# An attention and two-MoE kernel on one core: the first MoE's sums laid out by model dimension, the second MoE's tokens staged by a table

## The chip, the core and the metric

The kernel runs on one core of a Trainium2 chip. A core has TensorE (PE, with its weight loads shown apart as PEld), VectorE (DVE), ScalarE (ACT), GpSimd (POOL) and SyncE (SP), which issues most transfers. Matrix products read SBUF and write PSUM, which has eight banks of 128 x 512 numbers. The metric is the device time of one execution in microseconds (us).

## The reference

```python
# attention without a softmax over pairs: q, k, v are (4, 8, 576, 64)
q_s = softmax(q, axis=-1);  k_s = softmax(k, axis=2)
x = (q_s @ (k_s^T @ v))            # per head; then (2304 tokens, 512)
# first MoE: 4 experts, d_model 512, d_ff 1024, all tokens through all experts
p = probs / (probs.sum(-1) + 1e-9)
for e in range(4):
    out += p[:, e:e + 1] * (relu(x @ w1[e]) @ w2[e])
# second MoE layer: one expert, d_ff 2048
result = elu(out @ w_in) @ w_out   # w_in and w_out are given in float64
```

## The kernel before, in words

Every factor is split into a high and a low part (`fp32r`), and each product is three matmuls: high x high, high x low, low x high. The first expert of the first MoE ("unit 0") is computed plainly, beside the attention: for a block of 256 tokens `first` makes one 128-wide slice of the hidden layer, `second` adds it into the sums of the block, and `evacuate` moves the finished sums into `accs` in SBUF, scaled by the token's probability. Hooks (`at(n, ...)`) put the attention's and other work between these matmuls; one hook comes after every 2048 columns.

The other three experts and the second MoE are 30 *steps* `i`, each of half an expert (index `s`, 0 to 9) and a third of the tokens (index `b` = `i` mod 3, 768 tokens in two halves `th` of TB = 384). Steps with `s` < 6 are the first MoE, those with `s` >= 6 the second. A step runs a Strassen-like scheme: the first layer is 14 products (7 for each of two halves `fp`; 6 matmuls of 384 columns each, line 1177) in four PSUM banks A, B, C, D, with sums of banks on VectorE (lines 1474 and 1485) and ScalarE. Of steps with `s` < 5 or `s` > 6 the second layer is seven products as well; they run one step later, in the places PLACES between the first-layer products (`second_product` for the first MoE, `turned_product` for the second). Steps with `s` = 5 and 6 have a plain second layer (`chunk` and `group`). The steps of `s` = 5 are 15, 16 and 17; each step's second layer runs in the step after it.

In `second_product` the hidden activations are the stationary operand, 128 tokens at a time, and the weights move: 3 token tiles x 6 matmuls of 256 columns for one product. The sums stand as (tokens, model dimension), and a token's probability is a scalar per partition: VectorE adds `probability x sum` into `accs` with three instructions of 128 x 256 (line 1425), and one of the seven products' parts goes through ScalarE (1420) and POOL (1421) instead. `chunk` does the same with 512 columns (lines 1263 to 1265, 1270). The second MoE needs its input as (model dimension, tokens), so `turn_steps` transposes `accs` on TensorE (line 970, 8 transposes and 2 copies by ScalarE for 256 tokens; 9 such pairs), makes the seven sums of quarters that its products need, splits them (`emit`, ScalarE, VectorE, POOL) and stores them to DRAM (`xs`), from where each step loads its operands (`ring_load`). `drain` pops one piece of up to two such streams after each first-layer product.

Every engine runs its instructions in the order in which the program writes them. VectorE's order within a step is thus fixed: the bank sums (1474 after product 2, 1485 after product 4), the ReLU parts (1355, 1360, 1369), the adds of the second products, the splitting of the next weights (777, 782, 783, 823) and the conversion of float64 weights (487 to 506). In the trace a first-layer product of one half `fp` cannot start overwriting a bank before the ReLU of the earlier content has read it.

## Time and profile before

| | before |
|---|---|
| time, median of 3 runs | 1180.96 us (1180.72 to 1181.03) |
| the profiled execution's own time | 1180.01 us |
| its span | 1178.2 us |
| TensorE matmuls, busy | 1161.9 us in 7551 |
| VectorE / ScalarE / POOL busy | 883.9 / 656.1 / 604.1 us |
| granted clock of TensorE | 1.00 over the whole span |

The span is what the trace covers; the execution's own time has 1.8 us around it. Matmul records overlap, since one matmul's end is modelled while the next already streams: what a matmul costs is the distance from its start to the next one's start, and a stretch can be 100% busy and still hold short waits.

### The profile page before, as it was taken

To read this page: it belongs to the slowest core of one execution; us is meant where nothing else is said; L and a number is where in the kernel's file an instruction comes from. 1 tells how busy PE (TensorE), PEld (TensorE's weight loads), DVE (VectorE), ACT (ScalarE), POOL (GpSimd) and SP (SyncE) were. 2 spreads that over 40 slices of the span, in tenths; PEclk is the share of its full clock that TensorE was granted. 3 is DMA by queue.
4 is the path that set the end of the run, shared out by engine and by line. 5 is a ranking of instruction groups with operands and counts; after the bars stand their busy time and mean duration, and the time that the engine had idled before them with its cause. 6 is when DMAs were issued, how large, how long until landed. Compare 5 with 4: busy or idle time off the path is not lost.

```text
span 1178.2 us, 21091 instructions
## 1 busy us (share of the span) xinstructions
PE 1161.9 (99%) x7551; PEld 1113.6 (95%) x7551; DVE 883.9 (75%) x1533; ACT 656.1 (56%) x1410; POOL 604.1 (51%) x582
## 2 busy tenths in 40 slices
PE   8999999999999999999999999999999999999998
PEld 6889898889999999999999999998999999999998
DVE  7878887555787787787787786576566779879876
ACT  7554544236455455455455453356767766767763
POOL 6522543027468468468468463246534645645643
PEclk9999999999999999999999999999999999999999
DMA  9446666846767767767777658798985465565462
GB/s 270 144 144 191 192 211 222 287 166 224 259 233 251 259 233 251 258 233 250 253 239 251 241 208 311 259 340 279 335 320 188 181 230 198 196 229 198 176 242 108
DMA packets 150345, 272.76 MB, mean 231 GB/s; under 512 B 12640, under 2 KB 74848, under 8 KB 150240
## 3 DMA queue, kind: packets, MB, share of 16 engines
q1 hardware_dynamic: 148512, 268.26, 66.1%
q10 hardware_dynamic: 1728, 3.15, 0.8%
q8 instruction: 60, 0.98, 0.3%
q14 instruction: 45, 0.37, 0.1%
HBM read 225.22 MB, written 46.14 MB: 230 GB/s over the span
## 4 chain that ended last, share of the span: by engine, by line
PE 80%; DVE 5%; ACT 2%; issue 1%; POOL 1%; DMA 0%; DVEq 0%; POOLq 0%; ACTq 0%
PE o L1403 19%; PE m L1177 17%; PE h L1177 17%; PE o L1312 8%; PE h L1035 4%; PE o L1035 4%; PE o L1283 1%; PE o L1284 1%; PE o L1285 1%; PE o L1264 1%; PE o L1265 1%; PE o L1263 1%; DVE accs L1321 1%; PE o L970 1%; DVE w1s L777 1%
## 5 line engine op out<-in xcount | busy, mean ns | idle before, releaser
L1177 PE MATMUL m<-xh,w1s 128*128 128x384 f32 x840 | 245.9, 337 | 1.3 <-DVE h L1474 0.8
L1177 PE MATMUL h<-xh,w1s 128*128 128x384 f32 x840 | 244.8, 337 | 1.9 <-DVE half L1233 0.9
L1177 PEld LDWEIGHTS m<-xh,w1s 128*128 128x128 f32 x840 | 154.2, 188 | 6.1 <-DVE gt L1360 2.2
L1177 PEld LDWEIGHTS h<-xh,w1s 128*128 128x128 f32 x840 | 154.8, 188 | 5.1 <-DVE half L1233 1.5
L1177 PE MATMUL h<-xl,w1s 128*128 128x384 f32 x420 | 140.7, 335 | 0.0
L1177 PE MATMUL m<-xl,w1s 128*128 128x384 f32 x420 | 140.6, 335 | 0.0
L1035 PE MATMUL o<-w2t,hpa 128*128 128x512 f32 x432 | 117.1, 399 | 1.0 <-ACT hpa L1066 0.5
L1035 PE MATMUL h<-xh,w1t 128*128 128x256 f32 (+1 forms) x512 | 110.9, 295 | 0.0
L1403 PE MATMUL o<-w2g,xh 128*128 128x256 f32 x540 | 90.4, 282 | 0.0
L1035 PEld LDWEIGHTS o<-w2t,hpa 128*128 128x128 f32 x432 | 75.7, 189 | 14.8 <-DVE hpa L1067 1.9
L1035 PEld LDWEIGHTS h<-xh,w1t 128*128 128x128 f32 x512 | 85.0, 189 | 4.8
L1403 PE MATMUL o<-w2g,hpa 128*128 128x256 f32 x540 | 89.0, 282 | 0.0
L1403 PE MATMUL o<-w2g,xl 128*128 128x256 f32 x540 | 87.3, 282 | 0.0
L815 POOL TENSOR_TENSOR w2g<-r,w2g 128x512 fp32r<-128x512 f32 x56 | 74.8, 1344 | 24.2 <-ACT w2g L814 24.2
L1425 DVE SCALAR_TENSOR_TENSOR accs<-o,pn,accs 128x256 f32<-128x256 f32 x180 | 75.7, 475 | 14.7 <-PE o L1403 14.1
L1177 PEld LDWEIGHTS h<-xl,w1s 128*128 128x128 f32 x420 | 79.2, 189 | 0.3
L1177 PEld LDWEIGHTS m<-xl,w1s 128*128 128x128 f32 x420 | 78.9, 188 | 0.5
L1403 PEld LDWEIGHTS o<-w2g,xh 128*128 128x128 f32 x540 | 78.0, 190 | 0.1
L1035 PE MATMUL h<-xl,w1t 128*128 128x256 f32 (+1 forms) x256 | 77.0, 301 | 0.5 <-DVE xl L413 0.5
L1403 PEld LDWEIGHTS o<-w2g,hpa 128*128 128x128 f32 x540 | 76.1, 190 | 0.1
L1403 PEld LDWEIGHTS o<-w2g,xl 128*128 128x128 f32 x540 | 75.7, 190 | 0.1
L1201 POOL TENSOR_TENSOR hpa<-gt,hpa 128x384 fp32r<-128x384 f32 x28 | 28.5, 1020 | 75.3 <-ACT hpa L1199 75.3
(357 smaller groups left out, 2960.3 us busy)
## 6 DMA issues: line engine op xcount, KB each, us to landing
xh<-xs SPq DMA_DIRECT2D x210, 384.0 KB, 5.5
xl<-xs SPq DMA_DIRECT2D x210, 384.0 KB, 6.1
r<-in_w_dram SPq DMA_DIRECT2D x56, 256.0 KB, 4.8
xs<-xh SPq DMA_DIRECT2D x21, 384.0 KB, 4.6
xs<-xl SPq DMA_DIRECT2D x21, 384.0 KB, 4.4
xs<-stage SPq DMA_DIRECT2D x29, 256.0 KB, 5.1
r<-scratch SPq DMA_DIRECT2D x24, 256.0 KB, 4.2
xs<-gt SPq DMA_DIRECT2D x21, 256.0 KB, 4.5
```

Of the source, the lines that this page charges most:

```text
L777: eng.tensor_tensor(out=dst(k, 1), in0=src(k), in1=dst(k, 0).bitcast(F32), op=ALU.subtract)
L815: nc.gpsimd.tensor_tensor(out=t[:, 1], in0=src, in1=t[:, 0].bitcast(F32), op=ALU.subtract)
L970: nc.tensor.transpose(t[:, d * P : (d + 1) * P], a[:, d * P : (d + 1) * P], ident)
L1035: nc.tensor.matmul(out, lhsT, rhs, **kw)
L1177: nc.tensor.matmul(dst, t[:, wl, c + dl, :], x[xl_][:, dl, :], start=(n == 0 and p < 2), stop=(n == 5), skip_group_check=True,)
L1201: eng.tensor_tensor(out=gl, in0=g, in1=gh.bitcast(F32), op=ALU.subtract)
L1263: nc.tensor.matmul(o, gh, w[:, 0, :], start=(f == 0), stop=False)
L1264: nc.tensor.matmul(o, gh, w[:, 1, :], start=False, stop=False)
L1265: nc.tensor.matmul(o, gl, w[:, 0, :], start=False, stop=(f == FS - 1))
L1312: nc.tensor.matmul(ym[m], l, r, start=(n == 0 and k in STARTS), stop=(n == 5), skip_group_check=True)
L1403: nc.tensor.matmul(o, l, r, start=(first_write and m == 0 and c != 1), stop=(m == 5), skip_group_check=True)
L1425: nc.vector.scalar_tensor_tensor(out=a, in0=sums[x][:, c * HALF_M : (c + 1) * HALF_M], scalar=pr, in1=a, op0=ALU.mult, op1=ALU.add)
```

## The change

Sums of the first MoE now stand as (model dimension, tokens), in the layout that the second MoE already used (`acc_turned`, `acc_half`). In unit 0, `chunk` (removed; `group` takes its steps) and `second_product`, the weights are the stationary operand and the tokens move: 384 columns in the steps, 256 or 512 in unit 0. The transposes (`turn`) go. A token's probability now lies along the free dimension: the normalised probabilities are transposed once (`p_turn`), stored to DRAM (`prow`), and loaded as rows spread over all partitions (`p_load`, 128 x 384, from SP's queue; two tiles `pb` for the steps). They are applied by whole-tile multiplications: for unit 0 on POOL in place (`p_scale`, ten instructions of 128 x 768 or less) and on VectorE for its last block; in `second_product` on VectorE, and the addition into `accs` then follows on VectorE (in place in PSUM) or on POOL (line 1460), by the rule in the diff.

The second MoE's tokens are staged by the table STAGING: for each first-layer product it names which pieces of the three 128-token columns run after it. Some places of weight preparation (`w1_steps`, `w2_fast`), of the staging buffers and the hooks of the steps with `s` = 5 (EARLY) move too.

```diff
+    prow = nc.dram_tensor("prow", (E * NTILE, P), F32).ap()
+    def acc_half(t):
+        return accs[:, 4 * t * TB : 4 * (t + 1) * TB].rearrange("p (m n) -> p m n", m=4)
...
+    def p_turn():
+        t = bank("m")[: NTILE * E, 0, :P]
+        nc.tensor.transpose(t, pe_, ident)
+        nc.scalar.activation(out=pcopy, in_=t, func=AF.Copy)
+        nc.sync.dma_start(out=prow, in_=pcopy)
+    def p_load(out, e, t):
+        nc.sync.dma_start(out=out, in_=prows[e : e + 1, t * TB : (t + 1) * TB].to_broadcast([P, TB]))
+    def p_scale(t, m, p, n=TB):
+        a = acc_half(t)[:, m : m + 2, :n]
+        nc.gpsimd.tensor_tensor(out=a, in0=a, in1=over(p[:, :n], 2), op=ALU.mult)
...
+        if p and 0 < s < S_FAST:
+            return {
+                -5: begin, -4: lambda: lo(0), -2: sums1, -1: lambda: hi(1), 4: lambda: lo(1), 5: sums2,
+                7: lambda: hi(2), 8: lambda: lo(2), 9: lambda: hi(3), 10: lambda: lo(3),
+            }
...
-        def turn(a):
-            t = bank("o")[:, 0, :]
-            for d in range(KD):
-                nc.tensor.transpose(t[:, d * P : (d + 1) * P], a[:, d * P : (d + 1) * P], ident)
-            nc.scalar.activation(out=a, in_=t, func=AF.Copy)
...
+    STAGING = {
+        5: "E10", 6: "S0", 7: "E11", 8: "S1 D10", 9: "E12 D11", 10: "S2 E20", 11: "S0 D12 E21", 12: "S1 D30",
...
+        def piece(m):
+            o = outs[u, bi][m // mb][:, m % mb * n : (m % mb + 1) * n]
+            w0, w1_ = (w[:, hl, m * P : (m + 1) * P] for hl in range(2))
+            first = f == 0 and m % mb == 0
+            matmul(o, w0, gh, start=first, stop=False, skip_group_check=True)
+            matmul(o, w1_, gh, start=False, stop=False, skip_group_check=True)
+            matmul(o, w0, gl, start=False, stop=(f == FPU - 1), skip_group_check=True)
...
+    for i in range(NB * (S_FAST + 1)):
+        for t, (j, n) in enumerate(((i, 18 if i else 23), (i + 1, 2))):
+            e, b = 1 + STEPS[i][0] * FS // FPU, STEPS[i][1]
+            at2(j, n, lambda e=e, t=t, b=b: p_load(pb[:, t], e, 2 * b + t))
...
     def group(i, th, m):
...
+        if s < S_MOE:
+            nc.vector.tensor_tensor(out=o, in0=o, in1=pb[:, th], op=ALU.mult)
+            nc.vector.tensor_tensor(out=a, in0=o, in1=a, op=ALU.add)
...
     def second_product(i, k):
...
+        for m in range(2):
+            n = 0
             for fp in range(2):
-                gh, gl = (y[:, js] for y in parts_of(i, op, fp))
-                for l, r in ((gh, t[:, 0, fp]), (gh, t[:, 1, fp]), (gl, t[:, 0, fp])):
+                gh, gl = parts_of(i, op, fp)
+                w = t[:, :, fp, m * P : (m + 1) * P]
+                for l, r in ((w[:, 0], gh), (w[:, 1], gh), (w[:, 0], gl)):
...
         elif k == 3:
+            nc.vector.tensor_tensor(out=sums["X"], in0=sums["Y"], in1=sums["s5"], op=ALU.add)
-            for c in range(3):
-                a, pr = target(1, 1, c)
-                cs = slice(c * HALF_M, (c + 1) * HALF_M)
-                nc.scalar.activation(out=r[:, cs], in_=sums["s5"][:, cs], func=AF.Copy, scale=pr)
-                nc.gpsimd.tensor_tensor(out=a, in0=r[:, cs], in1=a, op=ALU.add)
         elif k in GOES:
-            for c in range(3):
-                a, pr = target(*GOES[k], c)
-                nc.vector.scalar_tensor_tensor(
-                    out=a, in0=sums[x][:, c * HALF_M : (c + 1) * HALF_M], scalar=pr, in1=a, op0=ALU.mult, op1=ALU.add
-                )
+            th, mh = GOES[k]
+            a, p = acc_turned(b, th, mh), over(pb[:, th], 2)
+            tt = nc.vector.tensor_tensor
+            if k == 5:
+                o = sums["X"]
+                tt(out=o, in0=sums["Y"], in1=sums["s5"], op=ALU.add)
+            if k == 4 and (i + 2) % NB or k == 6 and (i + 1) % NB == 0:
+                tt(out=o, in0=o, in1=p, op=ALU.mult)
+                tt(out=a, in0=o, in1=a, op=ALU.add)
+            else:
+                r = tmp.tile([P, 2, TB], F32, tag="ql", name="part")
+                tt(out=r, in0=o, in1=p, op=ALU.mult)
+                nc.gpsimd.tensor_tensor(out=a, in0=r, in1=a, op=ALU.add)
```

How the order of instructions moves is shown at three places. First TensorE, in unit 0 (`o` are the block's sums, `w2t` its second-layer weights, `hpa` the hidden activations, `x6` six equal instructions in a row), before:

```order
L1035 MATMUL h<-xh,w1t 128x256
L306 MATMUL m<-accs,ek 64x65 x10
L1035 MATMUL o<-w2t,hpa 128x512 x6
L1035 MATMUL h<-xh,w1t 128x256
L1035 MATMUL h<-xl,w1t 128x256
```

The sums of two 128-token tiles take three matmuls each. In the changed program the same place of TensorE reads:

```order
L1068 MATMUL h<-xh,w1t 128x256
L312 MATMUL m<-accs,ek 64x65 x10
L1068 MATMUL o<-hpa,w2t 128x256 x12
L1068 MATMUL h<-xh,w1t 128x256
L1068 MATMUL h<-xl,w1t 128x256
```

Six matmuls of 512 columns become twelve of 256; what moves is now the activations. The same in one product of `second_product` (`w2g` the weights; `xh`, `gx`, `hpa` places of the activations), before:

```order
L1403 MATMUL o<-w2g,xh 128x256 x3
L1403 MATMUL o<-w2g,gx 128x256 x3
L1403 MATMUL o<-w2g,xh 128x256 x3
L1403 MATMUL o<-w2g,gx 128x256 x3
L1403 MATMUL o<-w2g,xh 128x256 x3
L1403 MATMUL o<-w2g,gx 128x256 x3
L1177 MATMUL m<-xh,w1s 128x384
L1177 MATMUL m<-xl,w1s 128x384
```

The tail of three x3 pairs shows that each token tile takes six matmuls. The same product on TensorE in the changed program:

```order
L1434 MATMUL o<-xh,w2g 128x384 x3
L1434 MATMUL o<-hpa,w2g 128x384 x3
L1434 MATMUL o<-xh,w2g 128x384 x3
L1434 MATMUL o<-hpa,w2g 128x384 x3
L1231 MATMUL m<-xh,w1s 128x384
L1231 MATMUL m<-xl,w1s 128x384
```

Eighteen matmuls of 256 columns become twelve of 384. Next VectorE, in the second half of step 2 (`b` = 2), from product 1 of `fp` = 1 to product 5; before:

```order
L493 TENSOR_SCALAR y<-x_3510 128x512
L1474 TENSOR_TENSOR m<-h,extra 128x384
L497 SCALAR_TENSOR_TENSOR y<-x_3510,y 128x512
L1425 SCALAR_TENSOR_TENSOR accs<-o,pn,accs 128x256 x3
L503 SCALAR_TENSOR_TENSOR ce<-x_3510,ce 128x512
L1485 TENSOR_TENSOR h<-h,extra 128x384
L1355 SCALAR_TENSOR_TENSOR xh<-h,xh 128x384
L506 SCALAR_TENSOR_TENSOR y<-y,ce 128x512
L777 TENSOR_TENSOR w1s<-r,w1s 128x512
L1360 SCALAR_TENSOR_TENSOR gt<-m,gt 128x384 x2
L1369 TENSOR_TENSOR gt<-gt 128x384
```

The three additions of 1425 come as soon as their product is done. After, on VectorE from the same place (1506 and 1517 are the bank sums 1474 and 1485; 1394 and 1399 the ReLU parts 1355 and 1360; 1453 and 1459 the sum and the multiplication of a second product; 493 to 512 the conversion; 810 the weight split 777):

```order
L499 TENSOR_SCALAR y<-x_3811 128x512
L1506 TENSOR_TENSOR m<-h,extra 128x384
L503 SCALAR_TENSOR_TENSOR y<-x_3811,y 128x512
L1453 TENSOR_TENSOR o<-o,m_3749 128x2x384
L1459 TENSOR_TENSOR part<-o,extra 128x768
L509 SCALAR_TENSOR_TENSOR ce<-x_3811,ce 128x512
L1517 TENSOR_TENSOR h<-h,extra 128x384
L1394 SCALAR_TENSOR_TENSOR xh<-h,xh 128x384
L512 SCALAR_TENSOR_TENSOR y<-y,ce 128x512
L810 TENSOR_TENSOR w1s<-r,w1s 128x512
L1399 SCALAR_TENSOR_TENSOR gt<-m,gt 128x384 x2
L1408 TENSOR_TENSOR gt<-gt 128x384
```

One group of three additions became a sum and a multiplication of 768 columns. Last POOL in the same half step (1421 the additions of the second product, 1338 and 1348 low parts of activations, 788 and 789 weight sums), before:

```order
L1421 TENSOR_TENSOR accs<-m5p,accs 128x256 x3
L1338 TENSOR_TENSOR hpa<-gt,hpa 128x384 x2
L1338 TENSOR_TENSOR xl<-gt,xl 128x384
L788 TENSOR_TENSOR r<-r 128x256
L789 TENSOR_TENSOR r<-r 128x256
L1348 TENSOR_TENSOR xl<-gt,xl 128x384
L1338 TENSOR_TENSOR gx<-gt,gx 128x384
L777 TENSOR_TENSOR w1s<-r,w1s 128x512
```

The three additions of the step stand at the head. After, on POOL from the middle of `fp` = 0 (1460 the additions, 1377 and 1387 the low parts, 821 and 822 the weight sums):

```order
L1460 TENSOR_TENSOR accs<-part,accs 128x768
L1377 TENSOR_TENSOR xh<-gt,xh 128x384
L1377 TENSOR_TENSOR hpa<-gt,hpa 128x384 x2
L1377 TENSOR_TENSOR xl<-gt,xl 128x384
L1460 TENSOR_TENSOR accs<-part,accs 128x768
L821 TENSOR_TENSOR r<-r 128x256
L822 TENSOR_TENSOR r<-r 128x256
L1387 TENSOR_TENSOR xl<-gt,xl 128x384
L1460 TENSOR_TENSOR accs<-part,accs 128x768
L1377 TENSOR_TENSOR gx<-gt,gx 128x384
L1460 TENSOR_TENSOR accs<-part,accs 128x768
L810 TENSOR_TENSOR w1s<-r,w1s 128x512
```

Before, three additions of 256 columns stand in the step; now four of 768 do, spread over it, two of them right ahead of the weight sums and of the next weight split.

## Rows read from the trace of the kernel before

**Rows 1.** The page, busy time of each engine.

```profile
PE 1161.9 (99%) x7551; PEld 1113.6 (95%) x7551; DVE 883.9 (75%) x1533; ACT 656.1 (56%) x1410; POOL 604.1 (51%) x582
```

**Rows 2.** Windows: end of unit 0, steps 2, 3, 4, 18; engines' busy us.

```profile
core 0: us, PE busy (x) PEld busy (x) DVE busy (x) ACT busy (x) POOL busy (x), PEclk, DMA share, GB/s
205.00:257.70 52.70, 52.70 (x259) 44.64 (x259) 31.31 (x48) 15.57 (x28) 6.34 (x5) 1.00 0.71 247
308.60:338.20 29.60, 29.60 (x212) 29.60 (x211) 24.44 (x40) 15.11 (x32) 14.61 (x15) 1.00 0.71 247
338.20:368.10 29.90, 29.90 (x211) 29.45 (x210) 24.00 (x43) 16.40 (x36) 22.03 (x20) 1.00 0.69 241
368.10:397.80 29.70, 29.70 (x212) 29.70 (x212) 22.39 (x41) 15.51 (x33) 19.57 (x18) 1.00 0.72 246
...
792.60:827.40 34.80, 34.47 (x183) 30.64 (x181) 22.07 (x36) 22.45 (x50) 22.73 (x27) 1.00 0.90 296
```

**Rows 3.** Timeline of TensorE, one second product of the first MoE.

```profile
start us, us, engine line op out<-in xcount [idle before <-releaser]
608.47 0.52 PE L1403 MATMUL o<-w2g,xh 128*128 128x256 f32 x3
...
610.62 0.34 PE L1177 MATMUL m<-xh,w1s 128*128 128x384 f32 x1
```

**Rows 4.** Timeline of TensorE, one `group` of the second MoE, twelve matmuls.

```profile
900.39 0.33 PE L1283 MATMUL o<-xl,w2s 128*128 128x384 f32 x1
...
902.47 0.33 PE L1177 MATMUL h<-xh,w1s 128*128 128x384 f32 x1
```

**Rows 5.** Timeline of TensorE, the transposes of one 256-token pair.

```profile
737.46 1.04 PE L970 MATMUL o<-ident,accs 128*128 128x128 f32 x8
738.25 0.48 PE L1263 MATMUL o<-w2s,xl 128*128 128x512 f32 x1
```

**Rows 6.** Timeline of TensorE, one `chunk`, twelve matmuls.

```profile
727.72 0.39 PE L1263 MATMUL o<-w2s,xl 128*128 128x512 f32 x1
...
730.48 0.33 PE L1177 MATMUL m<-xh,w1s 128*128 128x384 f32 x1
```

**Rows 7.** Timeline of TensorE in unit 0: second layer, then a first layer.

```profile
205.55 1.55 PE L1035 MATMUL o<-w2t,hpa 128*128 128x512 f32 x6
206.93 0.28 PE L1035 MATMUL h<-xh,w1t 128*128 128x256 f32 x1
...
208.37 1.55 PE L1035 MATMUL o<-w2t,hpa 128*128 128x512 f32 x6
```

**Rows 8.** Timeline of VectorE in step 2 and into step 3.

```profile
322.97 1.51 DVE L777 TENSOR_TENSOR w1s<-r,w1s 128x512 fp32r<-128x512 f32 x1
...
333.38 1.25 DVE L1425 SCALAR_TENSOR_TENSOR accs<-o,pn,accs 128x256 f32<-128x256 f32 x3
334.56 0.68 DVE L503 SCALAR_TENSOR_TENSOR ce<-x,ce 128x512 uint16<-128x512 uint16 x1
335.16 0.55 DVE L1485 TENSOR_TENSOR h<-h,extra 128x384 f32<-128x384 f32 x1
336.65 0.56 DVE L1355 SCALAR_TENSOR_TENSOR xh<-h,xh 128x384 fp32r<-128x384 f32 x1 [0.94 <-ACT gt L1354]
...
337.73 0.68 DVE L777 TENSOR_TENSOR w1s<-r,w1s 128x512 fp32r<-128x512 f32 x1
338.33 1.01 DVE L1360 SCALAR_TENSOR_TENSOR gt<-m,gt 128x384 f32<-128x384 f32 x2
```

**Rows 9.** Timeline of POOL in step 2.

```profile
322.76 1.17 POOL L1338 TENSOR_TENSOR xh<-gt,xh 128x384 fp32r<-128x384 f32 x1 [3.59 <-ACT xh L1337]
323.89 2.58 POOL L1421 TENSOR_TENSOR accs<-m5p,accs 128x256 f32<-128x256 f32 x3
```

**Rows 10.** Timeline of TensorE's weight loads, first product of step 3.

```profile
339.39 0.19 PEld L1177 LDWEIGHTS m<-xh,w1s 128*128 128x128 f32 x1 [0.29 <-DVE gt L1360]
```

**Rows 11.** Timeline of VectorE, a 768-column addition from PSUM.

```profile
354.57 0.97 DVE L1415 TENSOR_TENSOR o<-o,m 128x768 f32<-128x768 f32 x1 [0.80 <-PE o L1403]
355.44 0.55 DVE L1355 SCALAR_TENSOR_TENSOR gx<-m,gx 128x384 fp32r<-128x384 f32 x1
```

**Rows 12.** One line's instructions: 768 columns on POOL, ns min/median/max.

```profile
L678 POOL TENSOR_TENSOR sum<-sum,xl x6: 1831/1850/2446, 121.8 to 194.3; 128x768 f32<-128x768 f32 x6
```

More of the change, by code (lines that the diff above doesn't have):

```diff
@@ L941, in staged @@
             stage[-1:] = two(tmp, "ek")
-        if now >= -SH and not more_places:
+            spare.append(stage[-2])
+        if now >= -SH - 3 and not more_places:
             y = gt.rearrange("p k n -> p (k n)").bitcast(F32R)
@@ L946, in staged, with stage_steps @@
         if now >= 0 and any(isinstance(t, str) for t in stage):
-            stage[:] = two(stg, "r") + [t for t in stage if not isinstance(t, str)]
-        if now >= 14 and len(stage) == 7:
+            stage[:] = two(stg, "r") + [t for t in stage if not isinstance(t, str) and t is not spare[0]]
+        if now >= 14 and len(stage) == 6:
             stage[:0] = two(stg, "r")
+        if now >= SH - 2 and len(spare) == 1:
+            spare.append(extra[:, TB : TB + DM].bitcast(F32R).rearrange("p (l n) -> p l n", l=2))
+            stage[:0] = spare[1:]
         t = stage.pop(0)
         stage.append(t)
-        if t == "extra":
-            return extra[:, TB : TB + DM].bitcast(F32R).rearrange("p (l n) -> p l n", l=2)
         return tmp.tile([P, 2, 2 * P], F32R, tag=t, name="staged") if isinstance(t, str) else t
-    def turn_steps(b, c):
-        j1, j2 = 6 * b + c, 6 * b + c + 3
-        a1, a2 = acc(j1), acc(j2)
-        q4 = {"B11": a1[:, : 2 * P], "B21": a1[:, 2 * P :], "B12": a2[:, : 2 * P], "B22": a2[:, 2 * P :]}
+    def stage_steps(b, c):
+        cs = slice(c * P, (c + 1) * P)
+        q4 = {f"B{mh + 1}{th + 1}": acc_turned(b, th, mh)[:, :, cs] for th in range(2) for mh in range(2)}
+        a1, a2 = (acc_half(2 * b + th)[:, :, cs] for th in range(2))
         stores = []
@@ L1072, in first, with evacuate @@
             hs[u, bi, f] = (gh[:, part], gl[:, part])
-    def evacuate(u, j, o):
-        if j % 2 and j >= NTILE - 4:
-            nc.vector.tensor_scalar(out=acc(j), in0=o, scalar1=pn[:, j, 0:1], scalar2=None, op0=ALU.mult)
-        else:
-            nc.scalar.activation(out=acc(j), in_=o, func=AF.Copy, scale=pn[:, j, 0:1])
+    def evacuate(bi, k, o):
+        t0, n = blocks[0][bi]
+        mb = 512 // n
+        o = o.rearrange("p (m n) -> p m n", m=mb)
+        t = t0
+        while t < t0 + n:
+            h, c = divmod(t, TB)
+            size = min(TB - c, t0 + n - t)
+            a = acc_half(h)[:, k * mb : (k + 1) * mb, c : c + size]
+            x = o[:, :, t - t0 : t - t0 + size]
+            if bi == len(blocks[0]) - 1:
+                nc.vector.tensor_tensor(out=a, in0=x, in1=over(pb[:, h % 2, c : c + size], mb), op=ALU.mult)
+            else:
+                nc.scalar.activation(out=a, in_=x, func=AF.Copy)
+            t += size
     def second(u, bi, fs):
@@ L1093, in second_ @@
         w = w2t[u, f]
-        def piece(j):
-            o = outs[u, bi][j]
-            js = slice(j * P, (j + 1) * P)
-            matmul(o, gh[:, js], w[:, 0, :], start=(f == 0), stop=False)
-            matmul(o, gh[:, js], w[:, 1, :], start=False, stop=False)
-            matmul(o, gl[:, js], w[:, 0, :], start=False, stop=(f == FPU - 1))
-            if f == FPU - 1:
-                evacuate(u, t0 // P + j, o)
-        return [lambda j=j: piece(j) for j in range(nj)]
+        mb = 512 // n
+        def piece(m):
[5 more added lines that the diff above has]
+            matmul(o, w0, gl, start=False, stop=(f == FPU - 1), skip_group_check=True)
+            if f == FPU - 1 and m % mb == mb - 1:
+                evacuate(bi, m // mb, outs[u, bi][m // mb])
+        return [lambda m=m: piece(m) for m in range(KD)]
     for step in START.split():
@@ L1149, in gslot @@
         return t[:, :TB], t[:, TB:]
-    idle, held = [0, 1, 2, 3, 4, 5, 6, 7, 12, 13, 8, 9, 10, 11], {}
+    idle, held = [0, 1, 2, 3, 4, 5, 6, 7, 13, 8, 9, 10, 11, 12], {}
     def take(*key):
@@ L1248, in elu, with group @@
             pend.append(rest_s4)
[L1250 removed]
+    def group(i, th, m):
         s, b = STEPS[i]
[L1253 removed]
         if sums:
@@ L1256, in chunk @@
             psum_o(4, 1)
-        o = bank("o")[:, 0, :]
-        for f in range(FS):
-            gh, gl = (t[:, js] for t in parts_of(i, c // 3, f))
-            if c % 3 == 2:
-                drop(i, c // 3, f)
-            w = w2s[s, f]
-            nc.tensor.matmul(o, gh, w[:, 0, :], start=(f == 0), stop=False)
-            nc.tensor.matmul(o, gh, w[:, 1, :], start=False, stop=False)
-            nc.tensor.matmul(o, gl, w[:, 0, :], start=False, stop=(f == FS - 1))
-            tick()
-        a = acc(j)
-        if s < S_MOE:
-            e = 1 + s * FS // FPU
-            nc.vector.scalar_tensor_tensor(
-                out=a, in0=o, scalar=pn[:, j, e : e + 1], in1=a, op0=ALU.mult, op1=ALU.add
-            )
-    def group(i, th, m):
-        s, b = STEPS[i]
         o = bank("o")[:, 0, :TB]
```

124 lines of the change are left out of this document (64 added, 60 removed), and 2 rows, old and new, of the table STAGING.

## The prediction

> **What bounds the kernel now.** The page's first part comes first: TensorE is busy for 99% of the span and VectorE for 75% [rows 1]. The stage table says the same of single steps, 29.60 to 29.90 us of matmuls in steps of that length [rows 2]. Yet "busy" hides short waits, since records overlap; so I went to the timeline and took distances between starts. Most of TensorE's stream runs at an even distance, so that the price of every added or removed matmul can be read off. Waits stand at few places, and the one that matters here is in the first product of steps 3, 6, 9, 12 and 15: the weight loads show 0.29 us behind VectorE's line 1360 [rows 10]. TensorE's granted clock is 1.00 in each of these stretches, the upper of its two levels, and nothing in the change lets it idle long. So the time is TensorE's stream of some 1,160 us, plus the places where VectorE's list of work falls behind it. I price the stream first and then those places.
>
> **What TensorE's stream gains and loses.** There are five terms.
>
> Second products of the first MoE: 15 steps x 7 = 105. Before, eighteen matmuls of 256 columns take from 608.47 to 610.62, 2.15 us [rows 3]. After, they are twelve of 384 columns with weights stationary, which is exactly what a `group` of the second MoE does already: 900.39 to 902.47, 2.08 us [rows 4]. The columns are the same (4,608); what goes is the small fixed cost of six matmuls. 105 x 0.07 = 7.3 us gained.
>
> Transposes: eight take from 737.46 to 738.25, 0.79 us [rows 5]; nine such groups go, 7.1 us gained. One transpose of 72 columns is added in unit 0, at most 0.1 us by the same row (0.79 / 8).
>
> Steps of `s` = 5: eighteen chunks at 2.76 us (727.72 to 730.48) [rows 6] are 49.7 us; 24 groups at 2.08 us are 49.9 us. 0.2 us lost.
>
> Unit 0: in each of 7 blocks x 8 slices, six matmuls of 512 columns (205.55 to 206.93, 1.38 us) become twelve of 256. Twelve of 256, with other weights each, stand right behind them: 206.93 to 208.37, 1.44 us [rows 7]. 56 x 0.06 = 3.4 us lost. The last block, of 512 tokens, keeps its count and width.
>
> Sum: -7.3 - 7.1 + 0.1 + 0.2 + 3.4 = -10.7 us.
>
> **What the other engines get.** Prices: an instruction of 768 columns with one input in PSUM costs VectorE 0.87 us (354.57 to the next start at 355.44) [rows 11]; three of 256 cost 1.18 us (333.38 to 334.56) [rows 8]; 768 columns on POOL, both inputs in SBUF, take 1.85 us [rows 12], three of 256 took 2.58 [rows 9].
>
> VectorE per step before: 4 x 1.18 + 0.87 = 5.6 us. After: the five sums and multiplications plus one for k = 5 are six, and the in-place additions make it 6, 7 or 8 by `b`: 6 in steps with `b` = 2 (5.2 us), 7 with `b` = 1 (6.1), 8 with `b` = 0 (7.0). Per three steps, +1.5 us on 24.44 + 24.00 + 22.39 = 70.8 us [rows 2], against about 87.7 us of TensorE. POOL per three steps: nine additions x 1.85 = 16.7 us for 3 x 2.58 = 7.7, +9.0 us on 56.2 [rows 2]. Both stay under 83%, so neither becomes the bound by its sum. ScalarE loses work (the scalings of line 1420, the copies behind the transposes). These changes lie beside TensorE's work unless an order makes TensorE wait.
>
> The additions in unit 0 lie in its last fifth, where POOL is busy 6.34 of 52.70 us [rows 2]: at most ten at 1.85 us are hidden there, and would cost up to 18.5 us were that room gone. The probability rows move 128 x 384 numbers each, some 45 loads; DMA's share is 0.69 to 0.73 in the steps [rows 2]. They stand on SP's queue ahead of operand loads, but the multiplication that each waits for was written one or two products earlier, and it lands several products before its use: taken as nothing. (Its bounds: 0, and the 0.9 us that the multiplication takes if every wait of SP showed, times 30 = 27 us; operand loads are issued seven products ahead, so the first.)
>
> **The one chain that I price.** In steps with `b` = 2 VectorE works through splits of the next weights, a conversion and second products; then product 1 of the next step must wait until line 1360 has read the bank. Before, that read runs from 338.33 and TensorE waits about 0.3 us for it [rows 8, 10]. The list behind it has no slack but one 0.94 us wait for ScalarE [rows 8]. In the change the last second product before it (k = 5) takes 2 x 0.87 instead of 1.18, +0.56; k = 2 and k = 4 take 0.87 for 1.18, -0.31 each. So by its own work the list is as long as before. But TensorE arrives 5 x 0.07 = 0.35 us earlier, and POOL now runs additions of 1.85 us in the same stretch. That matters to VectorE: a weight split (line 777, both inputs in SBUF) that began at 322.97 while POOL worked until 323.93 took 1.51 us, and one at 337.73 with POOL idle 0.68 [rows 8, 9]. So each such instruction that meets a POOL addition can wait for the rest of it. Laying the order of both engines out with these prices, I find two such meetings that the old order didn't have, at the conversion after k = 4 (499, 503) and around k = 5 (509), about half an addition (0.9 us) in all; more does not follow, since VectorE then waits for TensorE or ScalarE. The added wait is thus 0.35 us if no meeting counts, 1.25 us if both do; I take 0.8 us, five times: 4.0 us.
>
> The Trainium skill's page "SBUF — State Buffer", section "SBUF: two separate sides", says that VectorE and GpSimd share a port pair as an exclusive lock held for a whole instruction, where VectorE's instruction has two SBUF inputs; it speaks against handing POOL longer additions. By it the sum would take the upper end, 6.3 us here; by the row, which shows a wait of 0.8 us for one instruction, the middle.
>
> In the steps of `s` = 5, sixteen instructions of 384 columns (at most 0.55 us each by line 1485 [rows 8], 8.8 us) replace six of 512 columns. In step 18 VectorE is busy 22.07 of 34.80 us [rows 2] and the step shrinks by 2.9 us; even with nothing taken off, 30.9 of 31.9. ScalarE's copies behind the transposes go. TensorE's waits there are 0.33 us in step 18 [rows 2]; I let all of them grow by 0.7 us (bounds: -1, if they went with the transposes, and +2).
>
> Sum: -10.7 + 4.0 + 0.7 = -6.0 us. On the profiled execution's own 1180.0 us that is 1174.0; its run is 1.0 us under the median of the three, so the median I forecast is 1181.0 - 6.0 = 1175.0 us.
>
> **The rivals.**
>
> Nothing is given back. The meetings fall where VectorE waits anyway, and the later places of the weight steps take the old waits away as well. For it: VectorE idles 5 to 7 us in each step [rows 2]. Against it: that idle time lies mostly elsewhere in the step than in this chain. Time: 1181.0 - 10.7, less up to 5 x 0.3 of old waits: 1168.8 to 1171.5.
>
> The gain is taken back everywhere. Not one transition in three but each has a wait of about 0.5 us more (`b` = 0 has most on VectorE, +1.4 us, and 22.03 us of POOL already [rows 2]): 15 x 0.5 + 4.0 = 11.5, time about 1181. Against it: my layout of `b` = 0 and `b` = 1 leaves 0.7 us or more before the read of line 1360 is needed.
>
> Slower: POOL's additions hold VectorE up in all steps. The mechanism is that of the meetings, its place the first-layer products 1 and 6, its price up to 1.85 us per addition. It decides from 0.9 us lost per step (10.7 and 2.4 us more, over 15 steps). With half of the nine additions in three steps met in full: 4.5 x 1.85 / 3 = 2.8 us a step, 42 us lost, 1212 us; with 1.2 us a step, 1188. POOL's queue is part of it: late low parts would stop a second product. It is the rule of the Trainium skill's page "SBUF — State Buffer", section "SBUF: two separate sides", taken to its end.
>
> The change doesn't shorten TensorE's stream, because twelve matmuls with fresh weights are paced by weight loads in unit 0 or with stationary weights of the second products. Against it: both forms stand in the rows at 0.12 and 0.17 us a matmul with fresh weights. I give it 1 in 100, within the slower ones.
>
> **How the numbers follow.** No change can be told from 0.2%, 2.4 us. Chances: partly given back, 1171.5 to 1178.6, 0.53 (own range 1172.5 to 1178.0 by the ends 0.35 and 1.25 us); nothing given back 0.22; taken back everywhere, within 0.2%, 0.15; slower 0.10. Faster is thus 0.75. The range reaches from 1169.5, inside the second case, to 1181.0, the middle of the third, and leaves out 2 in 10.
>
> **What would show it.** In the profile after: second products at 2.08 us, no instruction of line 970's kind, twelve matmuls of 256 at 1.44 us in unit 0; steps of about 29.2 us where they were 29.6; steps 17 and 18 shorter by about 2.5 us. The first or second product of steps 3, 6, 9, 12 and 15 shows a wait for the read of a bank by line 1399, near 1.1 us where it was 0.3. If it shows none, I was wrong on the meetings; if waits for 1399, 1506 or 1517, or for POOL's low parts, stand in all steps, the third or fourth case holds. POOL should stand at about 665 us (604 and 15 / 3 x 9.0, and up to 18.5 in unit 0), VectorE near 895 us. Wrong in kind would be a stream of matmuls with other distances than these rows show.

## The result, and the profile after

The changed kernel takes 1192.08 us, median of 4 runs (1191.14 to 1193.76); the kernel before took 1180.99 us beside it (4 runs, 1180.72 to 1182.05). The ratio is 1.0094, 95% interval 1.0076 to 1.0111: slower by 11.1 us, where 6.0 us less were forecast. The profiled execution is the slowest of the four, 1193.76 us with a span of 1191.7, and the only one of them whose mean granted clock is below 1.00 (0.998).

The page's busy times, which answer [rows 1] (VectorE was forecast near 895 us, POOL at about 665):

```profile
PE 1158.8 (97%) x7258; PEld 1128.0 (95%) x7258; DVE 939.9 (79%) x1481; ACT 631.0 (53%) x1349; POOL 683.1 (57%) x591
```

Windows of steps 3, 4, 5 and 18 (`b` = 0, 1, 2 and 0), columns as in [rows 2]:

```profile
339.15:370.75 31.60, 29.96 (x170) 28.95 (x169) 27.72 (x35) 15.53 (x32) 24.80 (x20) 1.00 0.65 226
370.75:402.15 31.40, 29.97 (x170) 29.04 (x169) 25.57 (x37) 14.75 (x30) 22.38 (x17) 1.00 0.73 264
402.15:431.35 29.20, 29.20 (x170) 29.09 (x169) 25.25 (x34) 14.18 (x29) 20.90 (x16) 1.00 0.77 261
...
803.55:840.35 36.80, 33.58 (x181) 32.61 (x180) 27.69 (x48) 18.87 (x43) 21.91 (x26) 0.95 1.03 339
```

The step with `b` = 2 has the 29.20 us that were forecast. Those with `b` = 0 and 1, of 29.90 and 29.70 us in [rows 2], are now 31.60 and 31.40, and TensorE idles 1.64 and 1.43 us in them. VectorE's busy time over three steps rose from 70.8 to 78.5 us, POOL's from 56.2 to 68.1.

TensorE's stream itself is as forecast. One second product of the first MoE, and one of unit 0's (timeline of TensorE, columns as in [rows 3] and [rows 7]):

```profile
608.43 2.25 PE L1434 MATMUL o<-hpa,w2g 128*128 128x384 f32 x12
610.51 0.40 PE L1231 MATMUL h<-xh,w1s 128*128 128x384 f32 x1
```

```profile
206.85 1.60 PE L1068 MATMUL o<-hpa,w2t 128*128 128x256 f32 x12
208.29 0.28 PE L1068 MATMUL h<-xh,w1t 128*128 128x256 f32 x1
```

They take 2.08 and 1.44 us, start to next start. So the loss is waits. I add them up from the trace: each matmul's distance to the next start, less the median for its line and width, where that is over 0.04 us.

| waits, us | unit 0 | steps 0-2 | 3-14 | 15-19 | 20-29 and end | sum |
|---|---|---|---|---|---|---|
| before | 22.4 | 1.0 | 1.4 | 2.5 | 4.8 | 32.1 |
| after | 20.9 | 1.2 | 18.0 | 11.8 | 4.7 | 56.7 |

24.6 us more of waits in a span that is 13.5 us longer leave a stream shorter by about 11.1 us, where 10.7 was forecast. Of the 11.8 us in steps 15 to 19, 1.7 are matmuls at TensorE's lower clock (last section), which this one execution of the four has.

Who ended them, from the waits of TensorE (us in total, times, longest) in steps 3 to 14; the same view of the kernel before has no row:

```profile
PE h L1231 <- DVE m L1506: 4.5, 4, 1.1
PE m L1231 <- ACT h L1502: 4.4, 4, 1.3
PE m L1231 <- DVE w1s L810: 2.1, 4, 0.5
```

The first two are the bank sum after product 2 (TensorE waits ahead of product 4, in steps with `b` = 0) and ScalarE's copy of a bank after product 1 (it waits ahead of product 2, in steps with `b` = 1), once per three steps each. The timeline of VectorE ahead of the first, in the second half of step 3 (POOL's work in the same stretch follows):

```profile
353.35 1.01 DVE L1399 SCALAR_TENSOR_TENSOR gt<-h,gt 128x384 f32<-128x384 f32 x2
354.28 1.28 DVE L1408 TENSOR_TENSOR gt<-gt 128x384 f32<-128x384 f32 x1
...
358.87 1.24 DVE L499 TENSOR_SCALAR y<-x 128x512 int32<-128x512 int32 x1
360.03 1.78 DVE L861 TENSOR_TENSOR r<-r 128x512 f32<-128x512 f32 x1
361.73 0.95 DVE L1455 TENSOR_TENSOR o<-o,extra 128x768 f32<-128x768 f32 x1
362.72 0.96 DVE L1456 TENSOR_TENSOR accs<-o,accs 128x768 f32<-128x768 f32 x1
363.59 1.26 DVE L503 SCALAR_TENSOR_TENSOR y<-x,y 128x512 f32<-128x512 uint32 x1
364.78 0.55 DVE L1506 TENSOR_TENSOR m<-h,extra 128x384 f32<-128x384 f32 x1
```

```profile
352.91 2.23 POOL L1460 TENSOR_TENSOR accs<-part,accs 128x768 f32<-128x768 f32 x1 [1.06 <-DVE part L1459]
355.11 1.61 POOL L853 TENSOR_TENSOR w2g<-r,w2g 128x512 fp32r<-128x512 f32 x1
...
359.79 1.47 POOL L810 TENSOR_TENSOR w1s<-r,w1s 128x512 fp32r<-128x512 f32 x1
```

TensorE's weight loads wait for that last instruction:

```profile
365.38 0.19 PEld L1231 LDWEIGHTS h<-xh,w1s 128*128 128x128 f32 x1 [1.44 <-DVE m L1506]
```

From 351.3 on VectorE has no free moment but 0.42 us. Its own additions are in the list (1455 and 1456, 1.9 us where three of [rows 8] took 1.18), and other instructions are longer beside POOL: 1408 takes 1.28 us (0.55 without POOL's additions, e1 below), 861 1.78. The second wait, ten microseconds later, comes through ScalarE:

```profile
375.19 0.63 ACT L852 ACTIVATE w2g<-r 128x512 fp32r<-128x512 f32 x1 [1.53 <-DVE r L861]
375.72 0.47 ACT L1499 ACTIVATE extra<-m 128x384 f32<-128x384 f32 x1
376.09 0.48 ACT L1502 ACTIVATE h<-m 128x384 f32<-128x384 f32 x1
```

A weight copy waits 1.53 us for VectorE's weight sum, and the bank copy 1502 stands behind it; TensorE's weight loads wait 1.66 us:

```profile
376.63 0.19 PEld L1231 LDWEIGHTS m<-xh,w1s 128*128 128x128 f32 x1 [1.66 <-ACT h L1502]
```

### The profile page after: what moved, and what is told of

Read it like the earlier page. It is cut to its first block, busy times and chain, and to the rows that moved or that the text cites. A ratio compares the mean times of both kernels' runs of the same rounds, so it can differ in the third digit from the quotient of the medians.

```text
span 1191.7 us, 20487 instructions
## 1 busy us (share of the span) xinstructions
PE 1158.8 (97%) x7258; PEld 1128.0 (95%) x7258; DVE 939.9 (79%) x1481; ACT 631.0 (53%) x1349; POOL 683.1 (57%) x591
## 5 line engine op out<-in xcount | busy, mean ns | idle before, releaser
L1460 POOL TENSOR_TENSOR accs<-part,accs 128x768 f32<-128x768 f32 x45 | 88.9, 1976 | 60.2 <-DVE part L1459 53.1
L1068 PE MATMUL o<-hpa,w2t 128*128 128x256 f32 (+1 forms) x768 | 119.9, 300 | 0.7 <-ACT hpa L1099 0.4
L1068 PEld LDWEIGHTS o<-hpa,w2t 128*128 128x128 f32 x768 | 104.0, 191 | 5.9 <-DVE hpa L1100 1.0
L1434 PE MATMUL o<-xh,w2g 128*128 128x384 f32 x360 | 79.8, 334 | 0.0
L1434 PE MATMUL o<-hpa,w2g 128*128 128x384 f32 x360 | 78.4, 334 | 0.0
L1434 PE MATMUL o<-xl,w2g 128*128 128x384 f32 x360 | 77.9, 334 | 0.0
L1434 PEld LDWEIGHTS o<-xh,w2g 128*128 128x128 f32 x360 | 63.9, 188 | 0.1
L1434 PEld LDWEIGHTS o<-hpa,w2g 128*128 128x128 f32 x360 | 63.9, 188 | 0.0
L1434 PEld LDWEIGHTS o<-xl,w2g 128*128 128x128 f32 x360 | 63.7, 188 | 0.1
L1360 DVE TENSOR_TENSOR accs<-o,accs 128x768 f32<-128x768 f32 (+1 forms) x63 | 57.0, 905 | 5.6 <-PE o L1351 5.6
```

The lines of the kernel that those rows point to most:

```text
L1068: nc.tensor.matmul(out, lhsT, rhs, **kw)
L1360: nc.vector.tensor_tensor(out=a, in0=x, in1=a, op=ALU.add)
L1434: nc.tensor.matmul(o[:, m], l, r, start=(k < 2 and n == 0), stop=(n == 5), skip_group_check=True)
L1460: nc.gpsimd.tensor_tensor(out=a, in0=r, in1=a, op=ALU.add)
```

## The experiments

Eighteen kernels, timed beside the kernel before. Waits in us as above, from one profile each; the ratio is to the kernel before on the same chip.

| run | us, median | ratio (95% interval) | waits 3-14 | waits 15-19 |
|---|---|---|---|---|
| e1 no POOL additions | 1185.36 | 1.0031 (1.0019 to 1.0042) | 12.0 | 10.0 |
| e2 no VectorE additions | 1181.92 | 1.0008 (0.9999 to 1.0018) | 10.0 | 10.5 |
| f4 no additions | 1176.62 | 0.9968 (0.9959 to 0.9978) | 5.1 | 9.0 |
| e6 no additions, no scaling | 1171.10 | 0.9915 (0.9900 to 0.9930) | 0.0 | 6.7 |
| e3 all additions on POOL | 1188.95 | 1.0058 (1.0043 to 1.0073) | 14.1 | 9.6 |
| e5 additions in halves | 1190.15 | 1.0071 (1.0056 to 1.0086) | 14.5 | 10.4 |
| e4 old weight places | 1188.04 | 1.0050 (1.0033 to 1.0067) | 16.9 | 9.5 |
| e7 no group work | 1191.18 | 1.0082 (1.0067 to 1.0097) | 16.5 | 10.3 |
| e9 copies on ScalarE | 1191.73 | 1.0091 (1.0076 to 1.0106) | 19.0 | 9.8 |
| f2 one buffer less | 1195.25 | 1.0123 (1.0109 to 1.0137) | 18.8 | 9.9 |
| f3 one buffer more | 1192.33 | 1.0101 (1.0087 to 1.0114) | 17.9 | 7.6 |
| e8 rescaling | 1183.97 | 1.0029 (1.0017 to 1.0040) | 10.0 | 7.9 |
| e10 rescaling, placed | 1183.90 | 1.0022 (1.0012 to 1.0031) | 11.2 | 8.2 |
| e11 e10, old weight places | 1181.79 | 1.0006 (0.9996 to 1.0015) | 8.6 | 8.7 |
| e12 e10, copies on ScalarE | 1184.32 | 1.0024 (1.0013 to 1.0035) | 11.2 | 9.2 |
| f1 e11, where POOL idles | 1183.92 | 1.0028 (1.0016 to 1.0039) | 10.4 | 9.0 |
| h1 e11, spread | 1181.61 | 1.0008 (0.9999 to 1.0018) | 8.4 | 11.0 |
| h2 h1, copies on ScalarE | 1180.67 | 0.9999 (0.9990 to 1.0008) | 8.4 | 7.4 |

Two things set how finely the waits can be read. The edits of e7, e9, f2 and f3 leave steps 3 to 14 alone, and these show 16.5 to 19.0 us there for the changed kernel's 18.0; a difference of 1.5 us says little. And some 1.6 us of the last column (of 3-14 in e4) is TensorE at its lower clock after a wait in the changed kernel, e1, f4, e7, e11, e12 and f1, and not in the others.

### Which work makes the waits of steps 3 to 14

**e1.**

```diff
-                nc.gpsimd.tensor_tensor(out=a, in0=r, in1=a, op=ALU.add)
```

> Left out: POOL's additions of the second products of the first MoE (line 1460, 45 of 768 columns), so these parts never reach the sums; the multiplications by the probability stay on VectorE. In steps 3 to 14 the changed kernel waits 18.0 us on TensorE where the kernel before waited 1.5. Theory A (POOL's long additions hold up VectorE's instructions with two SBUF inputs): VectorE's lines 1408, 861, 499 to 512 fall back to about what they took before, the waits of steps 3 to 14 fall from 18 to under 4 us, and the time is 1176 to 1180 us. Theory B (VectorE's own added multiplications and additions make its list too long, wherever POOL works): the waits stay at 14 to 18 us and the time at 1189 to 1193 us.

Neither: 12.0 us stay, 6.0 went. One line's instructions (duration ns min/median/max) of the changed kernel, and then of e1, in steps 3 to 12:

```profile
L1408 DVE TENSOR_TENSOR gt<-gt x20: 545/998/1372, 340.9 to 631.0; 128x384 f32<-128x384 f32 x20
```

```profile
L1408 DVE TENSOR_TENSOR gt<-gt x20: 541/548/550, 341.4 to 626.7; 128x384 f32<-128x384 f32 x20
```

The lengthening of this line goes with POOL's additions. The same holds for VectorE's other work in sum: its 328 instructions in steps 3 to 14 that are no sum, scaling or addition of a second product take 234.1 us before, 254.8 after and 226.4 in e1, where POOL has less to do than before the change. Yet 861 stays long in e1 (median 1496 ns after 1778); it runs beside POOL's lines 1377 and 853 there. How much of the 6.0 us comes through VectorE and how much through POOL's own queue, which e1 shortens too, was not taken apart.

**e2.**

```diff
                 tt(out=o, in0=o, in1=p, op=ALU.mult)
-                tt(out=a, in0=o, in1=a, op=ALU.add)
```

> Left out: only VectorE's additions in place (line 1456, three per three steps, 0.87 to 0.96 us each); their multiplications stay in PSUM and reach no sum. POOL's nine additions stay. The run without POOL's additions kept 12.0 of 18.0 us of waits in steps 3 to 14, so theory A alone has fallen. Theory B (VectorE's own list): one addition stands right ahead of each late bank sum, so 3 x 0.9 us per three steps go: waits of steps 3 to 14 at 7 to 11 us, 1182 to 1186 us. Theory A (only POOL's work counts): 16 to 18 us of waits, 1190 to 1192 us.

8.0 us of waits go with only 15 instructions, 12 of them in steps 3 to 14: theory B holds for its share. Place counts here: these 12 are 11.5 us of VectorE's work, while e1 took 28.4 us off its other instructions for 6.0 us of waits. **f4** takes both away:

> Left out: POOL's additions (1460) and VectorE's (1456); all multiplications stay, so no second product reaches a sum. If the two shares of the waits in steps 3 to 14 add up (6.0 and 8.0 of 18.0 us): 3 to 5 us of waits stay, 1176 to 1179 us. If they share a cause (one list that is late, whichever work makes it so): 0 to 2 us or 7 to 9 us.

5.1 us are left of 18.0; shares of 6.0 and 8.0 would have left 4.0, so they nearly add up. **e6** takes the multiplications as well (lines 1455 to 1460):

> Left out: all multiplications by the probability and all additions of the second products (lines 1455 to 1460), on VectorE and POOL; only the sums 1446 and 1453 stay, so the four results of a step reach no sum. It shows what the steps cost when nothing of the new layout's work stands in the lists. If the waits come from this work (own list and what POOL holds up together): under 2 us of waits in steps 3 to 14, and 1173 to 1176 us. Rival D (the waits come from other moved places or the probability rows): above 6 us of waits, over 1179 us.

Windows of its steps 3 to 5:

```profile
340.40:369.50 29.10, 29.10 (x170) 29.10 (x169) 19.91 (x31) 16.04 (x34) 19.35 (x18) 1.00 0.75 250
369.50:398.60 29.10, 29.10 (x169) 29.10 (x169) 19.64 (x28) 14.00 (x29) 17.57 (x15) 1.00 0.81 278
398.60:427.70 29.10, 29.10 (x169) 29.10 (x169) 19.14 (x31) 14.05 (x29) 11.82 (x12) 1.00 0.77 254
```

No wait is left in steps 3 to 14: all of them come from the work of scaling and adding. The time is 10.0 us under the kernel before, with the 6.7 us of waits in steps 15 to 19 still in it.

**e3** and **e5** keep all that work and move or cut it:

```diff
-            if k == 4 and (i + 2) % NB or k == 6 and (i + 1) % NB == 0:
+            if False:
```

> All four additions of a step go to POOL, also the three per three steps that VectorE did in place (k = 4 and 6); the same sums. VectorE loses 3 x 0.87 us per three steps, POOL gains 3 x 1.85 us. Theory B (VectorE's own list is too long): four fifths of the waits of steps 3 to 14 go, 1179 to 1183 us. Theory A (POOL's additions hold up VectorE): what VectorE loses in own work it gets back in longer two-input instructions; between 1188 and 1197 us, waits in steps 3 to 14 of 12 to 22 us.

```diff
-                nc.gpsimd.tensor_tensor(out=a, in0=r, in1=a, op=ALU.add)
+                for m in range(2):
+                    nc.gpsimd.tensor_tensor(out=a[:, m], in0=r[:, m], in1=a[:, m], op=ALU.add)
```

> Each addition of line 1460 (768 columns) becomes two of 384; the same sums, the same columns on POOL, some 0.2 us more of POOL's time per pair. Theory A with the lock held for a whole instruction: VectorE gets in after half the time, its lengthening in steps 3 to 11 (16.6 us of instructions over nine steps) falls by a quarter to a half, and the time falls by 3 to 8 us, to 1184 to 1189. Theory A with bandwidth that is shared rather than a lock: no gain, 1191 to 1194. Theory B: no gain either, 1191 to 1193.

e3 is theory A's case: VectorE lost 15 additions, which alone were worth 8.0 us of waits, and POOL's 15 more gave half of it back (14.1). e5 shortened line 1408 to a median of 550 ns (longest 1419) and took 3.5 us of waits, but the time fell by only 1.9 us, between the two forms of theory A (3 to 8 us, and none) and hardly clear of the noise. It decides neither.

**e4** undoes the moved places of the weight preparation (the branch with `0 < s < S_FAST` goes, and T3 stands at 19 and 22 again).

> The places of the weight preparation (w1_steps, w2_fast) as in the kernel before; all else as changed. Rival C (the moved places put VectorE's weight work where the list has no room): 1180 to 1186 us, the waits of steps 3 to 14 under 8 us. Theories A and B: the waits move but stay within a few us of 18, 1189 to 1196 us.

Rival C fell: 16.9 us of waits, 15.3 without the clock's share. But the time is 4.0 us less than the changed kernel's, of which the waits of one profile show 3.4 (1.1 and 2.3): the moved places did not help.

### The steps of s = 5 and the staging

**e7** leaves out the two instructions behind each group (1322, 1323).

> Left out: in steps 15 to 18 the multiplication and addition behind each group of the steps with s = 5 (lines 1322 and 1323, 48 instructions of 384 columns), so the third expert's second half is missing in the sums. In steps 15 to 19 the changed kernel waits 11.8 us, the one before 2.5. If VectorE's work behind the groups makes them: 2 to 4 us of waits there and 1183 to 1186 us. Rival E (the staging, its copies on ScalarE and its stores): 9 to 12 us of waits stay, 1190 to 1193 us.

10.3 of 11.8 us stay: the groups' work is 1.5 us at most. In step 18 a chain was in sight, VectorE, then ScalarE:

```profile
808.98 1.22 DVE L1033 TENSOR_TENSOR stage<-accs,stage 128x512 fp32r<-128x512 f32 x1 [2.58 <-POOL stage L1024]
...
811.30 0.47 DVE L810 TENSOR_TENSOR w1s<-r,w1s 128x256 fp32r<-128x256 f32 x1
```

```profile
812.63 0.64 ACT L799 ACTIVATE w1s<-r 128x512 fp32r<-128x512 f32 x1 [6.00 <-POOL r L821]
813.17 0.48 ACT L1271 ACTIVATE half<-h 128x384 f32<-128x384 f32 x1
814.97 0.49 ACT L1272 ACTIVATE stage<-h 128x384 f32<-128x384 f32 x1 [1.32 <-DMA xs<-stage]
```

So **e9** copies on ScalarE:

```diff
-E3=lambda: emit(("T3", "B22"), a2, "h"),
+E3=lambda: emit(("T3", "B22"), a2),
```

> The changed kernel, with the nine copies of the staging that POOL makes (line 1024) on ScalarE instead. With the groups' work left out, 10.3 of 11.8 us of waits in steps 15 to 19 stayed, so rival E (the staging) is ahead. In step 18 VectorE waits 2.58 us at line 1033 for a copy by POOL that stands behind two differences (line 1039), and a sum of weights, ScalarE's weight copy (6.0 us idle) and its ELU come late behind it; three such waits are 9.0 us. If that queue makes the waits: steps 15 to 19 at 5 to 8 us, time 1186 to 1189 us. If the staging buffers' stores or ScalarE's own load make them: 10 to 14 us, 1190 to 1194 us.

Step 18's waits fell from 5.6 to 2.7 us, of which 1.7 is the clock, step 19's rose from 1.6 to 2.5, and the time did not move: the chain in sight does not set it. **f2** and **f3** change the buffers. In f2 a staged piece lands on `gt` while that holds float64 weights ahead of their conversion, and part of the second MoE's weights is lost; only its time bears on the argument.

> The changed kernel without the staging buffer that it takes from the row tile's space late in step 18 and after. If the buffers' stores make the waits of steps 16 to 19 (10.1 us): 1 to 4 us more there, 1193 to 1197 us. If the engines' own load makes them: within 1 us of the changed kernel, 1191 to 1193 us.

> The changed kernel without the groups' multiplications and additions (as in the run without them: the third expert's second half reaches no sum) and without their probability rows, and the space of the row tiles is a staging buffer from the start. Against 1191.2 us and 10.3 us of waits in steps 15 to 19 in that run: if the buffers' stores make them, 2 to 5 us less, 1186 to 1189 us; if not, within 1 us.

f2 is 3.2 us slower, as the buffers' theory said, but 1.6 us of it stand in step 20 and none in 16 to 19. f3 took step 18 from 4.1 (e7) to 1.2 us, of which 1.6 is the clock, and step 20 went from 0.0 to 1.9: its time is 1.1 us above e7's, within the noise of the two. Buffers shift these waits, and one more gains nothing. Why there are some 7 us of them even in e6 is not settled. The windows show the DMA engines full there (share 1.00 in step 17, 1.03 in 18), but the kernel before, with 2.5 us of waits, shows 1.04 and 0.90 in the same steps. No run took transfers away, and none put the old staging back.

### A version with less work

**e8** keeps the sums in units of the current expert's probability: a second product is added and no more, and between two experts POOL multiplies by the ratio.

```diff
+            x, y = (pe_[:, k * NTILE : (k + 1) * NTILE] for k in (e, e + 1))
+            nc.vector.reciprocal(out=psm, in_=y)
+            nc.vector.tensor_tensor(out=x, in0=x, in1=psm, op=ALU.mult)
...
+        nc.gpsimd.tensor_tensor(out=a, in0=a, in1=over(pb[:, th], 2), op=ALU.mult)
...
+            tt(out=a, in0=o, in1=a, op=ALU.add)
```

> The same result by another way: the sums are kept in units of the current expert's probability. A second product is only added (one instruction of 768 columns on VectorE); between two experts POOL multiplies the sums by the ratio of the probabilities (24 instructions of 768 columns in all, in place of 45 additions), and the groups of s = 5 apply the last probability. VectorE has six instructions of 0.87 us per step (5.2) where it had 6, 7 or 8, and before 5.6. If the whole list of VectorE decides (own work and what POOL holds up): waits of steps 3 to 14 of 0 to 6 us, 1176 to 1182 us, with the waits of steps 15 to 19 left as they are. If the moved places of the weights decide: over 10 us of waits and over 1186 us.

8.1 us faster than the changed kernel, still slower than before: 10.0 us of waits, of which 7.4 stand in steps 6, 7, 12, 13, which hold POOL's multiplications. **e10** moves these:

> The rescaling kernel with two places moved: POOL's multiplications for b = 1 at the head of steps 6 and 12, for b = 2 in steps 8 and 14 instead of 7 and 13 (where 2.7 and 1.7 us of waits stood, against 0.5 in steps 4 and 10), and the ratios of the probabilities later in unit 0. If meetings with POOL's long instructions make the waits where VectorE's list is full: waits of steps 3 to 14 from 10.0 to 4 to 6 us, unit 0 at 259.4 us as in the changed kernel (261.3 before this), 1176 to 1179 us. If place doesn't matter: 1182 to 1185 us.

A miss. In step 6 (429.2 to 460.1) POOL's four multiplications ran from 436.5 to 448.3 among its low parts, and late in the step ScalarE waited for one of those:

```profile
456.03 0.49 ACT L1407 ACTIVATE gt<-m 128x384 f32<-128x384 f32 x1 [3.19 <-POOL hpa L1398]
```

**e11** takes the old weight places too, **e12** the copies of e9:

> As the rescaling kernel with moved places, but with the weight preparation (w1_steps, w2_fast) at the places of the kernel before. With VectorE's own list as short as before and no additions on POOL, rival C says that the old places leave no more waits than before: steps 3 to 14 under 3 us and 1173 to 1176 us. Otherwise within 2 us of the kernel with the moved places.

> As the rescaling kernel with moved places, with the staging's nine copies on ScalarE instead of POOL. If the copies' queue on POOL makes the waits of steps 15 to 19 (8 us there): 3 to 5 us less, 1172 to 1176 us. If not: within 1.5 us of the kernel without that edit.

e11 is 2.1 us faster than e10, but its 8.6 us of waits in steps 3 to 14 are far from rival C's 3; e12 takes the same time as e10. **f1** and **h1** place POOL's multiplications twice more:

> The rescaling kernel with the old places of the weights and POOL's multiplications between two experts where POOL is idle: b = 0 in steps 5 and 11, b = 1 in steps 8 and 14, b = 2 late in steps 7 and 13; the ratios in two instructions instead of six. Steps 6, 7, 12 and 13 held 6.3 of the 8.6 us of waits in steps 3 to 14 of its predecessor, and there ScalarE waited 3.2 us for POOL's low parts behind the multiplications. If that queue made them: waits of steps 3 to 14 at 2 to 4 us and 1175 to 1178 us, faster than the kernel before. If the even halves of the experts hold the waits in any case: 1180 to 1182 us.

> The rescaling kernel with the old places of the weights; POOL's four multiplications of a third of the tokens are spread over a whole step each (b = 0 in steps 5 and 11, b = 1 in 6 and 12, b = 2 in 8 and 14). If it is the packing of POOL's long instructions that delays the low parts: waits of steps 3 to 14 at 5 to 7 us, 1177 to 1180 us, faster than the kernel before by 0.1 to 0.3%. If not: 1181 to 1184 us.

Both missed: f1 brought 1.4 us of waits into each of the steps 8 and 14, h1 kept 3.0 in each of the pairs 6-7 and 12-13. **h2** is h1 with the copies on ScalarE:

> The same with the staging's nine copies on ScalarE instead of POOL. If the copies' queue on POOL costs time: 1 to 3 us less than its sister. If the waits only move to other places of steps 16 to 20: within 1 us of it.

0.9 us less than h1, which the intervals do not tell apart, and at the time of the kernel before (0.9999). Its VectorE is busy 65.95 us over three steps, 4.9 less than before the change, and yet TensorE waits 1.0 us in steps 3 and 4 where it waited 0.3 in the kernel before. So VectorE's sum of work does not set these waits; which place does in the rescaling kernels stays open. No version with the whole result beat the kernel before; f4 and e6, which did, leave work out.

## Why the prediction was wrong

**The stream: right.** -10.7 us were forecast; 2.08 and 1.44 us per product are as priced, the profiles give about -11.1, and e6 stands 10.0 us under the kernel before.

**The chain that was priced: right in size.** Into steps with `b` = 0 the waits grew from 0.28 to 1.0 us (distances at 339.3 to 341.6 over the median), some 0.7 us each time where 0.8 was taken. Most of it shows one instruction earlier in the same list of VectorE, at the weight split that product 0 needs, and the read of 1399 ends the rest (weight loads, answering [rows 10]):

```profile
340.13 0.30 PEld L1231 LDWEIGHTS m<-xh,w1s 128*128 128x128 f32 x2 [0.83 <-DVE w1s L810]
...
341.06 0.19 PEld L1231 LDWEIGHTS m<-xh,w1s 128*128 128x128 f32 x1 [0.28 <-DVE gt L1399]
```

**The step that failed** is the sentence that "my layout of `b` = 0 and `b` = 1 leaves 0.7 us or more before the read of line 1360 is needed", and the rule ahead of it, "more does not follow, since VectorE then waits for TensorE or ScalarE". The other deadlines of a step were not laid out: the bank sum after product 2 (1506) and, through ScalarE's queue, the copy 1502. The waits stand there, about 1.3 and 1.5 us once in three steps each. The rival "slower" had the size: 16.6 us more in steps 3 to 14 are 1.4 us a step, past the 0.9 us from which it decides. It had part of the cause, since VectorE's own additions make 8.0 us of the waits and POOL's 6.0, and not the place: it named products 1 and 6, "taken back everywhere" the transitions between steps, and the waits stand ahead of products 4 and 2 and in no step with `b` = 2. Only "What would show it" named waits for 1506.

**VectorE's own list, mis-sized.** +1.5 us over three steps were forecast. The 21 instructions of 768 columns are busy 20.2 us where 18.0 stood before (groups by line), so +2.2. From start to start one takes the 0.87 us that were priced, and 0.98 to 1.06 when the next needs its result (361.73 to 362.72 above). The larger miss is that a sum over three steps prices no place: VectorE still idles 4 to 6 us in each of steps 3 to 5, and by e2 12 additions of 0.96 us, right ahead of a deadline, made 8.0 us of waits.

**POOL's meetings, mis-sized most.** Two meetings, 0.9 us per three steps, were forecast; VectorE's 78.5 - 70.8 - 2.2 = 5.5 us are longer instructions with the same work. e1 shows that they go with POOL's additions, line 1408 for one. The Trainium skill's page "SBUF — State Buffer", section "SBUF: two separate sides", says that the shared ports are held for a whole instruction; the trace agrees (last section), and the row with 0.8 us, on which the prediction put the middle, was one meeting of many. POOL grew by 11.9 us over three steps, for 9.0 forecast: its additions too are longer, 1976 ns in the mean for the 1850 of [rows 12].

**The steps of s = 5: outside their bounds.** 0.7 us (-1 to +2) were forecast for them; steps 15 to 19 gave 9.3, and step 18, forecast 2.5 us shorter, is 2.0 longer. 1.7 us of it is the clock in the profiled execution, which the prediction took as steady. 3.0 us in steps 15 and 16 go when second products are not scaled and added (e6), and 1.5 at most are the groups' (e7). The remaining 3 us or so moved with every edit of the staging, without an edit that removed them. The staging table was taken as free; that it makes these waits is not shown, and their cause is open.

**Unit 0 and the rows.** Unit 0 is 1.7 us longer (3.4 of stream, 1.5 of waits less); POOL's multiplications there are hidden. Probability rows held VectorE once, 1.5 us in step 17.

## What to carry to other kernels

When the bound engine gets shorter, every deadline of the others comes earlier: lay out each place where it waits for them, not only the one that waits now. On an engine with an order of its own, an instruction's price goes by the deadline that it stands ahead of: here 0.96 us ahead of one cost 0.7 us of waits (8.0 for 12), although the engine idled elsewhere in the step. Long POOL instructions on SBUF are also paid for on VectorE, by the instructions that meet them: those with two SBUF inputs, and in this trace some conversions with one.
